# Sketched attention feeding a swish MoE on one core: query features spread over partitions through DRAM, a smaller first chunk, key sums on GpSimd, one fixed order

## The chip, the cores and the metric

The kernel runs on one core of one Trainium2 chip. The metric is device time in microseconds (us) of one execution; executions of one kernel mostly agree within a few per cent (130.0 to 135.0 us in all runs of the kernel before), and each comes with the mean clock that TensorE (PE) was granted, as a share of full speed. Lower is better. The engines are PE (matrix multiply), VectorE (DVE), ScalarE (ACT), GpSimd (POOL), and SyncE (SP), which issues most DMAs, the copies to and from DRAM. In these kernels data lies in SBUF, and PE's results in PSUM. A transfer lands when its last byte has arrived. A run is called slow when it is over 1.5% above the fastest run of its kernel; the others are fast.

## The reference

Four batches of four heads of 1088 tokens, head dimension 32. The attention is linear: each token's 32 values are projected by two 8 x 32 sketches, and phi is the outer product of the two results (64 features). Its output, 4352 tokens of 128 values, goes through a swish MoE layer with 2048 hidden units.

```python
def phi(x):
    a = np.einsum('rd,bhsd->bhsr', S1, x)
    b = np.einsum('rd,bhsd->bhsr', S2, x)
    return np.einsum('bhsi,bhsj->bhsij', a, b).reshape(*x.shape[:-1], 64)
q_p, k_p = phi(q), phi(k)
kv  = np.einsum('bhsf,bhsd->bhfd', k_p, v)
z   = np.sum(k_p, axis=2)
num = np.einsum('bhsf,bhfd->bhsd', q_p, kv)
den = np.einsum('bhsf,bhf->bhs', q_p, z)[..., None] + 1e-06
x   = (num / den)                       # then (tokens, 128)
h   = x @ w_in                          # 128 -> 2048
out = (h / (1 + np.exp(-beta * h))) @ w_out
```

## The kernel before

The MoE is cut into *waves*: PE multiplies two blocks of 128 hidden units with 512 tokens (tile `wave`, two buffers), ScalarE applies Silu to 128 x 1024 elements (tile `g`), and PE adds them into `moeout`. There are 68 of them. Attention work stands between the waves: phi(q) has 64 features on partitions, so PE *spreads* both sketch factors, each value repeated eight times, into PSUM (`aps`, `bps`). ScalarE copies one to SBUF (`asb`) and VectorE multiplies the two (`qp`). phi(k) has tokens on partitions: one burst `kps`, a transpose `kab`, and a product `kp` for each head; `kvz` holds kv and z, `dps` the denominator, `nps` the numerator. The divide writes `xT`, which the waves read.

```python
def ab(a_of=None, b_of=None, pool_b=None):      # spread for one pair of heads
    ...                                         # [cut: 8 or 16 matmuls into aps, bps]
    if a_of is not None:
        nc.scalar.copy(out=ASB[a_of][:, :, :w], in_=aps[:, :, :w])
    if b_of is not None:
        def mult():
            nc.vector.tensor_tensor(out=QP[bb][...], in0=bps[:, :, :w], in1=ASB[b_of][:, :, :w], op=MUL)

def sum_z(b):                                   # kp summed over its nine groups of tokens
    nc.vector.tensor_tensor(out=z4, in0=kp[:, :, 1:5], in1=kp[:, :, 5:9], op=ADD)
    ...                                         # [cut: three smaller adds]

for b in range(1, B):                           # later batches, each step between waves
    turn_q(b, 1)
    slot(lambda: r_group((b, 1, 0), (b, 0, 0)), 1)
    zs = sum_z(b)
    slot(lambda: kv(b, [1, 2, 3, 4], zs), 1 if few else 2)
    slot(lambda: r_group((b, 0, 1), (b, 1, 0)), 1)
    ...                                         # [cut: the same for the other parts, den, num, divide]
```

For each engine but SyncE the program fixes the order of its instructions: the one in which it names them. Beta is broadcast to 128 partitions by a DMA of 1 MB.

## Time and profile before

| | before |
|---|---|
| median of 3 runs, us | 131.4 (130.27 to 131.69) |
| first Silu, us from the span's start | 23.0 |
| second divide of batch 0 | 31.1 |
| first divide of batches 1, 2, 3 | 52.1, 77.2, 98.9 |
| end of the last Silu | 125.0 |
| DMA | 12.4 MB |

The first lines are from the page of the profile: the span of 130.2 us in 40 equal slices, each digit the busy share of a slice in tenths; PEclk is the granted clock, and DMA the mean share of 16 DMA engines.

```profile
PE   5787999887889999999997999999999989888830
...
ACT  1303010876358767477777866687776798888930
...
PEclk9999999999999999999999999999999999999998
DMA  3999999999992320031000400500032050031232
```

The next are from the table of stretches. For each stretch it has its length, then the busy us of PE, PE's weight loads, DVE, ACT and POOL (with the number of instructions), then granted clock, DMA share and GB/s.

```profile
core 0: us, PE busy (x) PEld busy (x) DVE busy (x) ACT busy (x) POOL busy (x), PEclk, DMA share, GB/s
0.00:23.00 23.00, 18.98 (x248) 8.77 (x248) 12.49 (x36) 3.55 (x8) 8.75 (x20) 1.00 0.96 270
23.00:57.00 34.00, 30.80 (x378) 11.05 (x382) 27.29 (x49) 22.84 (x27) 2.33 (x5) 1.00 0.58 122
57.00:102.00 45.00, 42.84 (x501) 16.65 (x501) 28.83 (x54) 32.97 (x38) 0.00 (x0) 1.00 0.17 25
102.00:125.00 23.00, 19.90 (x96) 9.11 (x95) 2.23 (x4) 20.41 (x21) 0.00 (x0) 1.00 0.23 35
```

PE is busy 31 of 34 us in the second stretch and 43 of 45 in the third, at full clock, and ScalarE 20.4 of 23 in the fourth. VectorE is busy 27 of 34 us in the second. The chain of work that ended last, followed backwards and given as shares by engine, says the same: PE and VectorE, hardly any DMA.

```profile
PE 49%; DVE 22%; ACT 15%; DMA 5%; issue 5%; SPq 1%; ACTq 0%; DVEq 0%
```

### The profile page before, as it was taken

What the parts mean: (1) busy time and instruction counts of PE and PEld (TensorE: products, weight loads), DVE (VectorE), ACT (ScalarE), POOL (GpSimd) and SP (SyncE); (2) the same over time, 40 slices, a digit from 0 to 9 for tenths busy, and PEclk for the clock granted to TensorE, in tenths of its full rate; (3) what the DMA queues carried; (4) which work ended last, traced back from release to release, by engine and by line L of the source; (5) the groups of instructions that cost most, each with busy time, mean ns of one, the idle gap of its engine ahead of it and who ended that gap; (6) DMA issues with size and microseconds to landing.
All of it is one profiled execution on the core that took longest, in us unless ns stands there. A gap on an engine that the chain in (4) does not pass through costs nothing.

```text
span 130.2 us, 2977 instructions
## 1 busy us (share of the span) xinstructions
PE 113.1 (87%) x1216; PEld 45.9 (35%) x1216; DVE 71.3 (55%) x142; ACT 79.8 (61%) x92; POOL 11.1 (9%) x24
## 2 busy tenths in 40 slices
PE   5787999887889999999997999999999989888830
PEld 2132933222334342342432332443432333334620
DVE  2579119249799988997367579940737400200210
ACT  1303010876358767477777866687776798888930
POOL 3000399700000000000000000000000000000000
PEclk9999999999999999999999999999999999999998
DMA  3999999999992320031000400500032050031232
GB/s 110 304 187 275 358 353 314 208 249 203 235 210 83 56 30 0 5 54 29 5 0 10 71 5 0 81 0 5 0 49 36 0 80 1 0 58 25 35 48 40
DMA packets 24909, 12.42 MB, mean 95 GB/s; under 512 B 18992, under 2 KB 23104, under 8 KB 24896
## 3 DMA queue, kind: packets, MB, share of 16 engines
q1 hardware_dynamic: 24576, 12.19, 42.1%
q8 instruction: 9, 0.15, 0.5%
q10 hardware_dynamic: 320, 0.04, 0.2%
q14 instruction: 4, 0.03, 0.1%
HBM read 10.00 MB, written 2.23 MB: 94 GB/s over the span
## 4 chain that ended last, share of the span: by engine, by line
PE 49%; DVE 22%; ACT 15%; DMA 5%; issue 5%; SPq 1%; ACTq 0%; DVEq 0%
PE moeout L223 15%; ACT g L267 15%; PE wave L259 13%; PE kvz L406 5%; DMA q<-in_q_dram 5%; PE aps L369 4%; DVE kp L346 4%; PE dps L471 3%; DVE qp L388 3%; PE bps L369 2%; DVE rb L489 2%; DVE xT L516 2%; PE nps L506 2%; PE kps L327 2%; DVE qT L315 2%
## 5 line engine op out<-in xcount | busy, mean ns | idle before, releaser
L267 ACT ACTIVATE g<-wave 128x1024 f16<-128x1024 f32 x68 | 67.8, 1023 | 30.1 <-PE wave L259 29.7
L223 PE MATMUL moeout<-g,woutp 128*128 128x512 f16 (+1 forms) x144 | 40.1, 369 | 3.3 <-ACT g L267 3.1
L259 PE MATMUL wave<-xT,winp 128*128 128x512 f16 (+1 forms) x144 | 40.0, 367 | 0.6 <-ACT g L267 0.4
L223 PEld LDWEIGHTS <-woutp 128*128 128x128 f16 x144 | 11.4, 97 | 24.8 <-issue 18.8
L259 PEld LDWEIGHTS <-winp 128*128 128x128 f16 x144 | 13.8, 97 | 17.3 <-issue 3.4
L388 DVE TENSOR_TENSOR qp<-bps,asb 128x576 f32<-128x576 f32 (+1 forms) x16 | 11.3, 713 | 14.5 <-ACT g L267 8.8
L233 DVE STREAM_TRANSPOSE o_sb<-moeout 128x512 f32<-128x512 f32 (+1 forms) x9 | 6.1, 676 | 21.5 <-PE moeout L223 21.5
L369 PE MATMUL aps<-qT,s_165 32*64 32x288 f32 (+1 forms) x128 | 13.6, 448 | 3.1 <-ACT g L267 2.0
L379 ACT COPY asb<-aps 128x576 f32<-128x576 f32 (+1 forms) x16 | 9.8, 610 | 5.7 <-PE aps L369 4.6
L369 PE MATMUL bps<-qT,s_170 32*64 32x288 f32 (+1 forms) x128 | 12.1, 446 | 0.1
L346 DVE TENSOR_TENSOR kp<-kab 128x576 f32<-128x576 f32 (+2 forms) x20 | 11.6, 620 | 0.0
L406 PE MATMUL kvz<-kp,v 128*32 128x64 f32 (+1 forms) x288 | 9.1, 246 | 1.2 <-DVE qp L388 0.8
L147 PE MATMUL warm<-idle 128*128 128x512 f16 x23 | 7.6, 479 | 1.5 <-DVE hm L159 1.5
L369 PEld LDWEIGHTS aps<-qT,s_165 32*64 32x64 f32 x128 | 4.6, 138 | 10.5 <-ACT g L267 5.3
L406 PEld LDWEIGHTS kvz<-kp,v 128*32 128x32 f32 (+1 forms) x288 | 6.5, 124 | 4.5 <-issue 2.3
L516 DVE TENSOR_TENSOR xT<-nps,rb 128x576 f16<-128x576 f32 (+1 forms) x8 | 5.8, 722 | 1.8 <-PE nps L506 1.4
L190 POOL TENSOR_TENSOR winp<-w_in_sb,beta_bc 128x256 f16<-128x256 f32 x8 | 5.5, 721 | 13.6 <-DMA beta_bc<-in_moe_beta_dram 13.6
L482 DVE STREAM_TRANSPOSE dT<-dps 128x288 f32<-128x288 f32 (+1 forms) x8 | 3.7, 463 | 5.1 <-PE dps L471 5.1
L315 DVE STREAM_TRANSPOSE qT<-q 128x576 f32<-128x576 f32 (+1 forms) x8 | 5.8, 726 | 0.8 <-DMA q<-in_q_dram 0.8
L489 DVE STREAM_TRANSPOSE rb<-rc 128x576 f32<-128x576 f32 (+1 forms) x8 | 6.0, 745 | 0.3
L327 PE MATMUL kps<-kT,sk 64*32 64x288 f32 x64 | 3.9, 482 | 2.3 <-DVE kT L303 2.3
L506 PE MATMUL nps<-qp,nd 64*32 64x288 f32 (+1 forms) x128 | 5.5, 401 | 0.0
(56 smaller groups left out, 60.9 us busy)
## 6 DMA issues: line engine op xcount, KB each, us to landing
v<-in_v_dram SPq DMA_DIRECT2D x16, 144.0 KB, 9.2
k<-in_k_dram SPq DMA_DIRECT2D x3, 544.0 KB, 11.8
q<-in_q_dram SPq DMA_DIRECT2D x3, 544.0 KB, 11.0
out_dram<-o_sb SPq DMA_DIRECT2D x20, 64.0 KB, 2.0
w_in_sb<-in_moe_w_in_dram SPq DMA_DIRECT2D x2, 512.0 KB, 8.7
beta_bc<-in_moe_beta_dram SPq DMA_DIRECT2D x2, 512.0 KB, 9.3
w_out_sb<-in_moe_w_out_dram SPq DMA_DIRECT2D x2, 512.0 KB, 9.8
k<-in_k_dram SPq DMA_DIRECT2D x1, 288.0 KB, 2.8
```

Of the source, the lines that this page charges most:

```text
L223: nc.tensor.matmul(out=moe["acc"][:, :tw], lhsT=woutp[:, j, :], rhs=g[:, jj, :tw], start=(j == 0), stop=(j == NJ - 1),)
L259: nc.tensor.matmul(out=wv[:, jj * tw : (jj + 1) * tw], lhsT=winp[:, (j0 + jj) * P : (j0 + jj + 1) * P], rhs=xT[:, t0 : t0 + tw], start=Tru ...
L267: nc.scalar.activation(out=g, in_=wv, func=ACTF.Silu)
L315: nc.vector.transpose(out=qT_of[b][:, t0 : t0 + tn].rearrange("p t c s -> p (t c s)"), in_=q_t[b][:, 2 * t0 : 2 * (t0 + tn)].rearrange("p ...
L346: nc.vector.tensor_tensor(out=KP[b][:, h, j0:j1].rearrange("p j (i l) -> p j i l", i=R), in0=bass.AP(tensor=a0.tensor, offset=a0.offset, a ...
L369: nc.tensor.matmul(out=dst[64 * c : 64 * c + 64, m, : 32 * tn], lhsT=sx[rows, :], rhs=qT_of[bb][rows, t0 : t0 + tn, c, :], start=True, sto ...
L379: nc.scalar.copy(out=ASB[a_of][:, :, :w], in_=aps[:, :, :w])
L388: nc.vector.tensor_tensor(out=QP[bb][:, 2 * pr : 2 * pr + 2, 32 * t0 : 32 * t0 + w], in0=bps[:, :, :w], in1=ASB[b_of][:, :, :w], op=MUL,)
L406: nc.tensor.matmul(out=kvz[32 * h : 32 * h + 32, F * which : F * which + F], lhsT=v_t[b][:kr, h, j, :] if which == 0 else ones[:kr, :], rh ...
L489: nc.vector.transpose(out=rb[:, :tn].rearrange("p t c s -> p (t c s)"), in_=bass.AP(tensor=r0.tensor, offset=r0.offset, ap=[list(r0.ap[0]) ...
L506: nc.tensor.matmul(out=nps[32 * h : 32 * h + 32, c, :w], lhsT=ND[b][rows, 32 * h : 32 * h + 32], rhs=QP[b][rows, h, 32 * t0 : 32 * t0 + w] ...
L516: nc.vector.tensor_tensor(out=xT[:, o : o + 2 * w].rearrange("p (t c s) -> p c t s", c=2, s=32), in0=nps[:, :, :w].rearrange("p c (t s) -> ...
```

## The change

The intent is to take work off PE and VectorE while the DMA queues stand mostly idle (DMA digits of 0 to 5 in the second half). For batches 1 to 3 the two small factors of phi(q) are computed unspread in one burst (`qps`), copied (`qsb`) and written to DRAM (`qd`). Reads with repeated addresses bring them back spread over 128 partitions (`qe`), and VectorE multiplies the two. Batch 0's first chunk has 256 tokens, its second 832, so there are 72 waves: 4 of 256 tokens, 16 of 416, the rest of 512 or less. The kp sums and nine of twelve kp products of later batches go to GpSimd. PE broadcasts beta. The order of all engines, SyncE included, is one string of tokens.

```diff
-    q_chk = [(0, 9), (9, TP - 9)]
+    q_chk = {b: [(0, 9), (18, 8)] for b in range(B)}
+    q_chk[0] = [(0, 4), (8, 13)]
+    tok_chk = [(0, 256), (256, 416), (672, 416)]        # then 512s
...
+    def qps(b):
+        t = two("qps")
+        ...                                             # 8 matmuls, unspread
+        nc.scalar.copy(out=s, in_=t[:, :, : NJK * 32])
+        nc.sync.dma_start(out=d, in_=s.rearrange("p a w -> p (a w)"))      # qd, in DRAM
+        for n in range(2):
+            nc.sync.dma_start(                          # first factor: one read, 128 partitions
+                out=e[0].rearrange("p m a w -> p (m a w)"),
+                in_=bass.AP(tensor=d.tensor, offset=d0 + 64 * n * W, ap=[[4 * W, 16], [0, R], [1, 2 * W]]))
+            for c in range(2):                          # second factor: two reads, 64 partitions
+                nc.sync.dma_start(
+                    out=e[1][64 * c : 64 * c + 64].rearrange("p m a w -> p (m a w)"),
+                    in_=bass.AP(tensor=d.tensor, offset=d0 + (64 * n + 32 * c + 2) * W,
+                                ap=[[0, R], [4 * W, R], [1, 2 * W]]))
+    def qmul(b, n, m=None):
+        nc.vector.tensor_tensor(out=QP[b, n][:, ms], in0=e[0][:, ms], in1=e[1][:, ms], op=MUL)
...
     def sum_z(b):
-        nc.vector.tensor_tensor(out=z4, in0=kp[:, :, 1:5], in1=kp[:, :, 5:9], op=ADD)
+        eng = nc.gpsimd
+        eng.tensor_tensor(out=z4, in0=kp[:, :, 0:4], in1=kp[:, :, 4:8], op=ADD)
...
+    SEQ = """
+        a0b1 lv2 tk1 c0 W a1 c1 mB1 b0 mB0 tq1 lk3 dB iB qp1 W W nB xB W W kp1 ka1 o12 o13 W W
+        W W tk2 tq2 W W O11 W W O10 kp2 va1 W m10 W tk3 z1 W vb1 ka2 np1 W lq3 nz1 m11 qp2 W d1
+        ...                                             # [cut: three more lines; W is one wave]
+    """
```

(Cut: the beta broadcast, other names, the order of the loads.)

The two reads of `qe` differ. The source pattern of the first factor has 16 rows as its outermost dimension, that of the second has a repeat of 8 with stride 0.

## The prediction

> **What bounds it now (131.4 us).** ScalarE's timeline splits the run by its 68 Silu waves of 1.02 us.
> - 0 to 23.0 us: prologue. The DMA row is full; the chain of waits runs q load, transpose, kab, kp, then kvz at 12.87 us. The page names a DVE multiply, but I read the v load there. kvz to 16.9, then kvd, nd, den, reciprocal, divide, wave.
> - 23 to 57 us: 18 waves, 1.9 us each. The table of stretches has DVE busy 8.9 to 9.4 of each 10 us from 30 to 60: DVE-bound.
> - 57 to 102 us: 29 waves, 1.55 us each, PE busy 8.8 to 9.9 of 10: PE-bound. PE needs 0.87 us for a wave's four 512-column matmuls, plus attention.
> - 102 to 125 us: 1.10 us a wave, ScalarE-bound. Tail 5.2 us.
>
> **Removed.**
> - Per later batch, four bursts of 16 spread matmuls (about 2.8 us) become one burst like kps (0.72): PE saves about 6 us in all. Four asb copies (2.4 us) become one of 0.64: ScalarE saves 5.3. The four PSUM products (2.85 us) become two of 1152 elements, estimate 1.35 us each from the 1024-element add of 1.21: nothing saved.
> - DVE loses the kp sums (2.75 us a batch) and 9 of 12 kp products (0.74 each): about 15 us.
> - The 1 MB broadcast of beta leaves the saturated prologue; PE and two ScalarE copies make it. Less q lies in front of v.
>
> **Added.** About 7.1 MB of DRAM reads and 0.9 MB of writes. From the 290 to 380 GB/s seen, about 7 us per batch plus two landings; small stores land in 2.0 us here[...]. GpSimd: at 721 ns per 256 elements, a kp product costs about 1.6 us and a batch's sums about 5.7 (estimates), 31 us in all, mostly off the chain.
>
> **Where it lies on the path (estimates).**
> 1. Prologue: v about 10.8, kv done about 13.4, 128-column chain, but the second chunk's spread stands before the first wave on PE: first Silu about 18.3 (before 23.0).
> 2. Waves 2 to 4 wait behind qps of batch 1 on PE, which waits for q's load (about 21.3). Second chunk divided about 27; batch 0 is then complete (before: 31.8).
> 3. Its 16 waves of 832 columns, about 1.0 us each, end about 43. Batch 1's second spread read, queued behind q, v, k loads, lands about 40, its divide about 45.5: a short gap.
> 4. 32 waves with batches 2 and 3: PE 0.87 x 32 + 5.6 x 2 = 39 us; with before's 10% slack about 43 us, to 89 us.
> 5. 20 waves ScalarE-bound, 21 us, then tail about 4.4 (last store on two queues).
> Sum: **114 us, range 107.5 to 121.** Faster by over 2%: 0.95; within 2%: 0.04; slower: 0.01.
>
> **What would show it.** First Silu at 17 to 19.5 us; no wave for some us before 24 and near 45; in the middle 1.3 to 1.4 us a wave; DVE under 65 us busy, GpSimd about 40; DMA about 19 MB.
>
> **What would make it wrong.** Spread reads landing late and blocking DVE and PE, which run in a fixed order. [...] If middle waves reach 1.15 us, 108.

(Two passages are cut from it: what it compared its 2.0 us of a small store with, and one way to be wrong that its trace did not show. No term of the sum is among them: 89 + 21 + 4.4 us is still about 114. Its 0.87 us for a wave's four matmuls is read from the trace of the kernel before, where matmuls of 512 columns in a row start at 88.48, 88.70, 88.92 and 89.13 us, 0.216 apart.)

## The result

| | before | after | predicted |
|---|---|---|---|
| median, us | 131.55 (130.27 to 133.44, 4 runs) | 141.43 (140.17 to 142.38, 4 runs) | 114 (107.5 to 121) |
| first Silu | 23.0 | 24.6 | 17 to 19.5 |
| second divide of batch 0 | 31.1 | 36.1 | about 27 |
| first divide of batch 1 | 52.1 | 62.2 | 45.5 |
| first divide of batches 2, 3 | 77.2, 98.9 | 84.8, 106.4 | none |
| end of the last Silu | 125.0 | 136.4 | none |
| DVE, GpSimd busy | 71.3, 11.1 | 56.7, 38.8 | under 65, about 40 |
| DMA, MB | 12.4 | 19.3 | about 19 |

The change is slower: the ratio is 1.074, with a 95% interval of 1.061 to 1.087. Ratios here and below are the mean time of one kernel's fast runs over that of the other's in the same rounds, so they are not quite the ratios of the medians. The profiled execution took 142.4 us, 1.6% over the fastest; where times inside it are compared with those of another kernel, the time of that kernel's profiled execution is taken.

The same lines of the page (span 140.6 us):

```profile
PE   5989299369998976869997399993399989889870
...
ACT  2261042504768566225889158884027798898860
...
PEclk9999956856999999779999999999559999999998
DMA  2999999501589564849857349956700404004042
```

PE has slices of 2 and 3 in the prologue and three of 3 in the middle, the DMA row is now busy to slice 29, and before the tail the clock has four stretches at half speed (17.0 to 23.8, 27.3 to 34.1, 58.0 to 61.4 and 98.9 to 105.8 us in the record of the clock). Just before three of these PE was busy 0.2 of 2.9 us, 0.9 of 2.7 and 1.1 of 3.5; but before the one at 58.0 us it was busy 1.1 of 1.8, and 1.2 of 3.6 us from 77.3 to 80.9 brought no half clock. The table of stretches, cut at the first Silu and at the divides that let waves begin:

```profile
0.00:24.60 24.60, 19.42 (x290) 8.54 (x290) 12.10 (x42) 7.18 (x17) 11.97 (x31) 0.86 0.89 291
24.60:36.10 11.50, 8.20 (x70) 2.62 (x71) 5.48 (x8) 4.34 (x6) 0.00 (x0) 0.70 0.25 88
36.10:62.20 26.10, 22.46 (x240) 9.67 (x238) 16.27 (x22) 14.92 (x20) 17.15 (x13) 0.93 0.64 141
62.20:106.40 44.20, 35.07 (x391) 13.95 (x391) 18.20 (x30) 25.95 (x29) 9.66 (x10) 0.92 0.63 143
106.40:136.40 30.00, 26.48 (x140) 11.63 (x139) 4.22 (x6) 25.64 (x28) 0.00 (x0) 1.00 0.20 32
```

In the stretch from 62.2 to 106.4 us PE is busy 35 of 44 us. The last long stretch, ScalarE busy 25.6 of 30, is as predicted. The chain that ended last, by engine and by line:

```profile
DMA 35%; PE 31%; ACT 10%; DVE 10%; issue 6%; SPq 5%; ACTq 1%; DVEq 0%
DMA qe<-qd 30%; ACT g L352 8%; PE moeout L318 8%; PE wave L343 6%; PE dps L596 4%; SPq L494 3%; PE kvz L528 3%; DMA beta<-in_moe_beta_dram 2%; DVE qp L509 2%; PE bps L442 2%; PE aps L442 2%; DVE rc L615 2%; ACT asb L453 1%; DMA qd<-qsb 1%; 
```

Nearly a third of the span now hangs on the reads `qe<-qd`. From the view of the waits (engine and line, what it waited for, us in total, times, longest):

```profile
DVE qp L509 <- DMA qe<-qd: 16.1, 4, 5.6
...
PE kvz L528 <- issue: 2.8, 1, 2.8
```

VectorE waited 16.1 us for these reads, four times. For each batch, from the issue of the first read to the start of the second product, the timeline shows 19, 17 and 17 us (36.12 to 55.25, 60.42 to 77.64, 82.58 to 99.44).

PE's timeline of the first 35 us (start, us busy, operation, and in brackets the idle time before and what ended it) shows two more losses. PE stands 2.8 us inside `kvz` where the profile finds nothing that it waits for ("issue"). Then the second chunk goes through one PSUM buffer, PE to ScalarE to VectorE to PE:

```profile
14.02 0.28 PE L528 MATMUL kvz<-kp,v 128*32 128x64 f32 x5
17.06 0.64 PE L528 MATMUL kvz<-kp,v 128*32 128x64 f32 x11 [2.77 <-issue]
...
24.72 0.93 PE L442 MATMUL aps<-qT,s 32*64 32x416 f32 x8 [0.38 <-ACT asb L453]
27.68 1.66 PE L442 MATMUL bps<-qT,s 32*64 32x416 f32 x8 [2.03 <-DVE qp L460]
30.49 1.61 PE L596 MATMUL dps<-qp,zb 128*32 128x416 f32 x8 [1.15 <-DVE qp L460]
32.03 1.21 PE L472 MATMUL qps<-qT,sq 64*32 64x288 f32 x16
```

`bps` takes 1.66 us here and `aps` 0.93, since the clock is at half from 27.3 to 34.1 us. SyncE's timeline shows that its queue is in order too (lines that start on SPq are issues; the time is from the first to the last of a group):

```profile
40.13 15.32 SPq L302 DMA_DIRECT2D out_dram<-o_sb  x8
55.50 0.47 SPq L117 DMA_DIRECT2D q<-in_q_dram  x1
56.07 0.38 SPq L483 DMA_DIRECT2D qd<-qsb  x1
...
79.40 0.59 SPq L147 DMA_DIRECT2D v<-in_v_dram  x1
80.09 0.54 SPq L483 DMA_DIRECT2D qd<-qsb  x1
```

The write `qd` of batch 2 stands behind the stores of an output chunk, that of batch 3 behind seven loads of v. Their data (`qsb`) was ready at 54.4 and 75.7 us.

### The profile page after: what moved, and what is told of

It is laid out like the page before. It is cut to its first block, busy times and chain, and to the rows that moved or that the text cites. A ratio compares the mean times of both kernels' runs of the same rounds, so it can differ in the third digit from the quotient of the medians.

```text
span 140.6 us, 2827 instructions
## 1 busy us (share of the span) xinstructions
PE 112.1 (80%) x1132; PEld 46.7 (33%) x1132; DVE 56.7 (40%) x106; ACT 78.1 (56%) x95; POOL 38.8 (28%) x53
## 3 DMA queue, kind: packets, MB, share of 16 engines
q1 hardware_dynamic: 26320, 19.07, 53.6%
## 4 chain that ended last, share of the span: by engine, by line
DMA 35%; PE 31%; ACT 10%; DVE 10%; issue 6%; SPq 5%; ACTq 1%; DVEq 0%
DMA qe<-qd 30%; ACT g L352 8%; PE moeout L318 8%; PE wave L343 6%; PE dps L596 4%; SPq L494 3%; PE kvz L528 3%; DMA beta<-in_moe_beta_dram 2%; DVE qp L509 2%; PE bps L442 2%; PE aps L442 2%; DVE rc L615 2%; ACT asb L453 1%; DMA qd<-qsb 1%; DVE qp L460 1%
## 5 line engine op out<-in xcount | busy, mean ns | idle before, releaser
L352 ACT ACTIVATE g<-wave 128x1024 f16<-128x1024 f32 (+2 forms) x72 | 67.4, 974 | 33.9 <-PE wave L343 33.5
L318 PE MATMUL moeout<-g,woutp 128*128 128x512 f16 (+3 forms) x160 | 41.9, 356 | 7.8 <-ACT g L352 4.2
L343 PE MATMUL wave<-xT,winp 128*128 128x512 f16 (+3 forms) x160 | 42.4, 362 | 1.2 <-DVE xT L643 1.2
L318 PEld LDWEIGHTS <-woutp 128*128 128x128 f16 x160 | 14.5, 99 | 31.6 <-issue 24.2
L328 DVE STREAM_TRANSPOSE o_sb<-moeout 128x512 f32<-128x512 f32 (+3 forms) x10 | 6.3, 630 | 33.3 <-PE moeout L318 30.4
L427 POOL TENSOR_TENSOR kp<-kab 128x576 f32<-128x576 f32 x9 | 11.5, 1301 | 24.8 <-DVE kab L419 21.8
L509 DVE TENSOR_TENSOR qp<-qe,qe 128x1152 f32<-128x1152 f32 x6 | 8.7, 1443 | 19.5 <-DMA qe<-qd 16.1
L596 PE MATMUL dps<-qp,zb 128*32 128x288 f32 (+2 forms) x64 | 6.7, 511 | 8.1 <-DVE qp L509 6.8
L550 POOL TENSOR_TENSOR z<-kp 128x1024 f32<-128x1024 f32 x3 | 7.0, 2350 | 11.9 <-DVE kp L427 11.8
L528 PE MATMUL kvz<-kp,v 128*32 128x64 f32 x288 | 6.7, 238 | 2.8 <-issue 2.8
L631 PE MATMUL nps<-qp,nd 64*32 64x288 f32 (+3 forms) x128 | 6.3, 458 | 0.0
```

The costliest lines, as they stand in the source:

```text
L318: nc.tensor.matmul(out=moe["acc"][:, :tw], lhsT=woutp[:, j, :], rhs=g[jj], start=(j == 0), stop=(j == NJ - 1),)
L328: nc.vector.transpose(out=o_sb[:, :nt, :].rearrange("p t d -> p (t d)"), in_=moe["acc"][:, :tw])
L343: nc.tensor.matmul(out=wv[:, jj // per, o : o + tw], lhsT=winp[:, (j0 + jj) * P : (j0 + jj + 1) * P], rhs=xT[:, t0 : t0 + tw], start=True, ...
L352: nc.scalar.activation(out=g[:, :, :gw], in_=wv[:, :, :gw], func=ACTF.Silu)
L427: (eng or nc.vector).tensor_tensor(out=KP[b][:, h, j0:j1].rearrange("p j (i l) -> p j i l", i=R), in0=cut(a0, [[32, jn], [1, R], [0, R]]), ...
L509: nc.vector.tensor_tensor(out=QP[b, n][:, ms], in0=e[0][:, ms], in1=e[1][:, ms], op=MUL)
```

## The experiments

All ran on the chip. Runs of one group shared a chip and the runs of the kernel before, whose fast runs had means of 130.9, 131.2, 131.6, 131.1 and 131.0 us in the five groups.

### Group 1: what the reads, GpSimd and the spread itself cost

**e1_wide**, wrong numbers: the second factor is read as one transfer with the first factor's pattern.

```diff
-            for c in range(2):
-                nc.sync.dma_start(out=e[1][64 * c : 64 * c + 64]..., ap=[[0, R], [4 * W, R], [1, 2 * W]])
+            nc.sync.dma_start(out=e[1]..., ap=[[4 * W, 16], [0, R], [1, 2 * W]])
```

> The second factor's two reads of 64 partitions become one read of 128 partitions with the address pattern of the first factor (the numbers are wrong on purpose; bytes unchanged). Theory A (narrow reads: these reads leave half of the DMA engines idle and run slowly on the rest, and their landing paces batches 1 to 3): the span from first read issue to the multiply of the second chunk falls from 19, 17 and 17 us to 8 to 10 us per batch, and the time falls to 118 to 127 us. Rival B (the TensorE clock that was granted at half speed after idle stretches sets the time) and rival C (GpSimd's sums and products hold VectorE and kvz up): no more than 3 us gained, 137 us or more.

Measured: 126.5 us (mean of the fast runs), ratio 0.967 (0.953 to 0.981). The same bytes come, in 11.0, 10.4 and 10.4 us a batch from the first packet to the end of the last, against 15.4, 14.7 and 14.7 in the changed kernel. That is 4.3 us a batch, three times. From the first issue to the second product it is now 16, 12 and 12 us, still not the 8 to 10 expected. The stretches of e1_wide between the same events (the columns as above):

```profile
34.20:56.80 22.60, 20.77 (x240) 9.57 (x239) 15.10 (x21) 15.04 (x20) 13.73 (x11) 1.00 0.71 166
56.80:90.70 33.90, 32.60 (x391) 13.61 (x391) 18.99 (x31) 25.71 (x29) 14.25 (x12) 1.00 0.82 185
90.70:120.70 30.00, 26.46 (x140) 11.65 (x139) 4.21 (x7) 25.77 (x28) 0.00 (x0) 1.00 0.20 32
```

The second row is the one to compare with 62.20:106.40 of the changed kernel. ScalarE runs the same 29 instructions in 33.9 us instead of 44.2, and PE is busy 32.6 of them. VectorE waits 5.1 us for the reads, not 16.1, and the chain hardly goes through DMA any more:

```profile
DVE qp L508 <- DMA qe<-qd: 5.1, 3, 3.2
...
PE 61%; ACT 17%; DVE 7%; issue 5%; DMA 4%; SPq 2%; ACTq 0%
```

So some 14 us of the miss lie in how the second factor is read, not in its bytes: 14.5 by the means of the fast runs, and 13.8 in the stages that hold reads. (The profiles differ by 1.8 us more before the first read at 36.1 us; runs with the same prologue have their first Silu between 22.9 and 24.6.)

**e1_k16**, wrong numbers: still two reads of 64 partitions each, but with 64 source rows outermost.

```diff
-    ap=[[0, R], [4 * W, R], [1, 2 * W]]
+    ap=[[W, 64], [1, 2 * W]]
```

> The second factor's two reads keep 64 partitions and the number of DMAs, but the source's outermost dimension is 64 rows instead of a repeat of 8 (wrong numbers on purpose). It parts two forms of theory A. If the count of DMA engines is the limit, the DMA row stays above 0.9 while reads run, a batch's reads take 11 to 13 us instead of 17 to 19, and the time is 126 to 134 us. If the 64 partitions alone are the limit, nothing changes: 138 us or more. Rivals B and C: no change.

Measured: one fast run of 126.35 us and three slow ones of 129.0 to 132.7; the packets of a batch took 10.3 to 11.0 us in the fast one. The two half-width destinations are therefore not what is slow; the outermost dimension of 8 is, in reads that SyncE issues (14.7 to 15.4 us a batch in the changed kernel). (This edit drops the repeat of addresses as well; e1_pool below keeps every address, and its packets are as fast, so the repeat alone is not the cause.) Below are 2 us near the end of a batch's reads in the changed kernel, where only narrow ones are left, and 2 us of e1_k16's reads (the columns as above): the DMA share is 0.54 against 1.04, and the rate 130 against 230 GB/s. A packet of 4.6 KB takes 0.32 us in the one and 0.34 in the other, so about half as many engines work at the same pace each (an estimate from the shares: 8.6 of 16, against all of them). Why these reads keep only half of them busy is not shown.

```profile
48.00:50.00 2.00, 1.85 (x10) 0.83 (x9) 1.67 (x2) 1.26 (x2) 1.18 (x2) 1.00 0.54 130
...
42.00:44.00 2.00, 1.88 (x16) 0.86 (x23) 0.00 (x0) 1.74 (x4) 1.99 (x1) 1.00 1.04 230
```

**kp_on_vector**: all kp products and sums of later batches back on VectorE, nothing else.

```diff
-            DO[f"o{b}{h}"] = lambda b=b, h=h: outers(b, [h], nc.gpsimd)
+            DO[f"o{b}{h}"] = lambda b=b, h=h: outers(b, [h], nc.vector)
...
-        eng = nc.gpsimd
+        eng = nc.vector
```

> The changed kernel with all kp products and sums back on VectorE. Rival C: faster by 5 us or more, since the 2 us stall of VectorE's add at 58 us and the wait for GpSimd's sums go. Theory A and rival B: within 2 per cent of the changed kernel (139 to 144 us), since VectorE is busy only 57 of 141 us and waits for the reads.

Measured: 141.0 us, ratio 1.078 (1.062 to 1.093), with VectorE busy 67.9 us and GpSimd 12.1. GpSimd's part is neither the cause nor a gain while the reads are slow.

**pe_spread**: later batches spread on PE as before, in the changed kernel's order.

```diff
-            DO[f"m{b}{n}"] = lambda b=b, n=n: qmul(b, n)
+            for pr in range(2):
+                DO[f"S{b}{n}{pr}"] = lambda b=b, n=n, pr=pr: spread_late(b, n, pr)   # ab, asb copy, product
```

(The string has S10, S11 and so on in place of m10, qp1 and so on.)

> phi(q) of batches 1 to 3 is spread on PE again, as in the kernel before, all else of the change kept (first chunk, GpSimd sums and products, beta by PE, fixed order). Theory A: no DRAM wait is left; 114 to 122 us, faster than the kernel before. Rival B: the prologue's half clock stays, so 133 us or more. Rival C: GpSimd's part stays, so slower than the kernel before (over 131 us).

Measured: 144.4 us, ratio 1.103 (1.087 to 1.120): a miss for theory A. The time lies in the ranges of rivals B and C, but neither is its cause by the other runs: e1_wide gained 14 us with GpSimd's part kept and most of the prologue's half clock too (17.1 us at half before 32 us), and kp_on_vector gained nothing. PE is busy 122.7 us and VectorE waits for the copy in 11 of the 12 spreads:

```profile
DVE qp L473 <- ACT asb L470: 23.2, 11, 3.1
```

The spread and the order can't be taken apart so simply. An order made for one big product a half batch is a bad one for four small chains. This run says nothing of what DRAM costs.

### Group 2: mending the reads, the clock, half of the spread, and sums alone

**e1_pool**: one word changed. GpSimd issues the second factor's reads.

```diff
             for c in range(2):
-                nc.sync.dma_start(
+                nc.gpsimd.dma_start(
                     out=e[1][64 * c : 64 * c + 64].rearrange("p m a w -> p (m a w)"),
```

> The changed kernel, correct, with the second factor's reads issued by GpSimd instead of SyncE; same addresses and sizes. If a read issued there is dealt to all 16 DMA engines whatever its outermost dimension (theory A then predicts the wide time): DMA row full while reads run, 127 to 134 us. If it is dealt to 8 as well: 139 to 145 us, no better than the change.

Measured: correct, 130.9 us, ratio 0.9975 (0.987 to 1.008). The packets of a batch took 10.1 to 11.1 us, as in e1_wide, with the outermost dimension still 8. The trace has a DMA share of 1.03 from 42 to 44 us. Why the issuing engine makes this difference is not shown. Issuing a batch's four reads held GpSimd for 2.25 us, about 0.56 each. This is the useful form of the same test, as its numbers are right, and it gains about 10 us on the changed kernel. It is 4 us short of e1_wide. In the profiles 1.5 us of that lie before the first Silu, where there are no reads, and 2.7 between the first divides of batches 2 and 3 (16.1 us against 13.4). Why is open. GpSimd's waits do not show that its products and sums hold the reads up:

```profile
POOL qe L494 <- DMA qd<-qsb: 16.9, 2, 13.6
...
POOL qe L494 <- DVE rc L617: 7.8, 1, 7.8
```

GpSimd's queue is in order (a kp product of batch 3, whose `kab` was written by 62.3 us, ran at 78.42, behind the reads issued from 76.19, though GpSimd had been idle for 3.3 us), but it sat idle before each batch's reads until the write had landed. The wait put down to `rc` is such a one too: SyncE's first read of that batch was issued at 55.8 us and GpSimd's at 56.3.

**wide_warm**: e1_wide with six dummy matmuls in the second chunk's chain.

```diff
-        a0b1 lv2 tk1 c0 W a1 c1 mB1 b0 mB0 tq1 lk3 dB iB ...
+        a0b1 lv2 tk1 c0 W a1 w3 c1 mB1 b0 w3 mB0 tq1 lk3 dB iB ...
```

> The wide-read kernel (wrong numbers, as e1_wide) plus six 512-column dummy matmuls on PE: three behind the spread of the second chunk's first factor and three behind that of its second, where PE was idle for 2.0 and 1.1 us and the clock was then at half for 6.8 us. If the half clock is a term of the loss (rival B as a second cause): the window of half clock from 25 to 32 us goes, the second chunk's divide comes 2 to 3 us earlier than at 34.2 us, and the time falls by 1.5 to 3 us against e1_wide (124 to 126). If only the chain's length counts: within 1 us of e1_wide.

Measured: 126.1 us, ratio 0.961 (0.949 to 0.973), so 0.4 us from e1_wide by these means, in other rounds; clock 0.986 instead of 0.929. The second chunk's chain is some 1.7 us earlier, and in the two profiled executions (125.0 and 126.8 us) that lead lasts to the end. The intervals overlap, so the half clock in that chain is worth at most about 2 us, and perhaps nothing.

**half_dram**: only the first factor goes through DRAM (with four buffers), the second is spread on PE.

```diff
-            for c in range(2): ...                      # the narrow reads
+    def bmul(b, n, pr):
+        bps = two("bps")
+        ab([("b", (n, pr), bps)], b)
+        nc.vector.tensor_tensor(out=QP[b, n][:, :, pr, :w], in0=bps[:, :, :w], in1=QE[b, n][0][:, :, pr, :w], op=MUL)
```

> A correct kernel without the narrow reads: the first factor comes through DRAM (rows as the outermost dimension, 128 partitions), the second is spread by PE into PSUM as in the kernel before and multiplied there; four buffers for the reads. Theory A: two reads a batch of 590 KB land within 5 to 7 us of the first issue; PE gets about 1.4 us a batch more than in e1_wide; 124 to 131 us, so equal to or up to 5 per cent faster than before. If any DRAM round trip is too slow in this order: over 135 us.

Measured: 137.8 us, ratio 1.050 (1.036 to 1.063), a miss. The wait for reads has become a wait for PE's bursts, which stand behind waves:

```profile
DVE qp L501 <- PE bps L442: 18.2, 12, 5.3
```

**before_zpool**: the kernel before with its kp sums on GpSimd, nothing else.

```diff
-        nc.vector.tensor_tensor(out=z4, in0=kp[:, :, 1:5], in1=kp[:, :, 5:9], op=ADD)
+        nc.gpsimd.tensor_tensor(out=z4, in0=kp[:, :, 1:5], in1=kp[:, :, 5:9], op=ADD)
```

> The kernel before with one part of the change alone: the kp sums on GpSimd. If VectorE bounds the stretch from 23 to 57 us as I read it, taking 2.75 us a batch off it saves 1.5 to 4 us (127 to 130). If the sums' longer latency on GpSimd (about 5.2 us, feeding the kvz products) costs as much, it is within 1 per cent.

Measured: 132.7 us, ratio 1.011 (0.996 to 1.027). VectorE was busy 63.7 us instead of 71.3, and nothing came of it. So the reading of the stage from 23 to 57 us as VectorE-bound is not confirmed: VectorE is busy there, but taking sums from it gained nothing. Whether VectorE was not the limit, or the sums' longer time on GpSimd took the gain back, this run does not part.

### Group 3: the prologue and the first chunk, on top of e1_pool

**late_loads**: seven loads, which nothing needs before about 22 us, wait until batch 0's last kp product (about 13 us), in a slightly changed order.

```diff
-    load_win(DFF // 2, DFF)
-    load_rows(k, k_t, 1, "k")
-    ...                                                 # and five more
     nc.gpsimd.tensor_copy(out=gate, in_=KP[0][:, H - 1, NJK - 1, :1])
+    nc.gpsimd.memset(w_in_sb[:, DFF // 2 : DFF // 2 + 1], 0.0)   # the load that follows must wait for this
+    load_win(DFF // 2, DFF)
+    load_rows(k, k_t, 1, "k")
+    ...
```

> The version with the second factor's reads issued by GpSimd (130.8 us), with seven loads that nothing needs before about 22 us (second half of w_in and w_out, k and q of batches 1 and 2, v of batch 1) held back until the last kp product of batch 0, about 13 us. Open: PE stops inside kvz of batch 0 for 2.4 to 3.8 us in every run and the trace shows nothing that it waits for; a 16 KB packet of an instruction fetch ends about 1.3 us before it goes on. Theory A, the fetch stands behind the queued loads: PE's gap falls below 1.5 us, the first Silu comes at 21.5 to 22.5 us instead of 24.6, time 128 to 129.5. Theory B, the gap has nothing to do with the loads: gap still 2.4 to 3.8 us, first Silu at 24 to 25, time 130 to 132.

Measured: 127.9 us, ratio 0.972 (0.966 to 0.978). PE's gap in `kvz` fell from 3.8 us (e1_pool) to 1.5, the first Silu came at 22.1 us instead of 24.6, and all that follows kept its pace and came 2.5 us earlier. PE's timeline of late_loads around the gap:

```profile
14.04 0.28 PE L521 MATMUL kvz<-kp,v 128*32 128x64 f32 x5
15.81 0.41 PE L521 MATMUL kvz<-kp,v 128*32 128x64 f32 x11 [1.49 <-issue]
```

In the packet records, a 16 KB packet of an instruction queue ends at 15.8 us in the changed kernel, 16.3 in e1_pool and 14.4 here, and PE goes on at 17.1, 17.7 and 15.8, each time 1.2 to 1.5 us later; so it is in all 15 profiles that have the gap. The moment at which PE goes on says more than the gap's length: in chunk512 below, with all loads queued, the gap is 1.3 us, but PE goes on at 17.1, as in the changed kernel. That the queued loads delay PE there is shown by this run. That PE waits there for instructions is a reading: it fits these and the later runs, but no run varied the fetch alone.

**early_waves**: the three waves left of the first chunk and batch 1's qps burst (in a buffer of the waves) stand in the idle time of the second chunk's chain.

```diff
-        a0b1 lv2 tk1 c0 W a1 c1 mB1 b0 mB0 tq1 lk3 dB iB qp1 W W nB xB W W kp1 ...
+        a0b1 lv2 tk1 c0 W a1 W c1 tq1 qp1 mB1 b0 W mB0 lk3 W dB iB nB xB W W kp1 ...
```

> The same version (130.8 us) with its loads as they were, but the order in the second chunk's chain changed: the three waves left of the first chunk and the qps burst of batch 1 stand between the spread bursts, where PE and ScalarE wait for each other (about 6 us of idle PE between 24 and 30 us). Theory A, this idle time is part of what the prediction missed: four Silu before 30 us instead of one before 33, batch 1's write to DRAM lands about 31 instead of 35.8, time 127.5 to 129. Theory B, the second chunk's chain alone sets what follows, or the middle stage is bound by PE's fixed order: time 130 to 132.

Measured: 135.7 us, ratio 1.031 (1.020 to 1.042): 5 us worse than e1_pool, where theory A expected 2 to 3 better and theory B no change. The divide came at 37.1 instead of 35.2 us, because the waves stood before the chain on PE. Then one kp product of batch 1 (the second `kp` line; its `kab` was written by 41.6 us) stood behind the output transpose of a wave chunk on VectorE's timeline, and GpSimd's sum behind it:

```profile
43.89 0.71 DVE L427 TENSOR_TENSOR kp<-kab 128x576 f32<-128x576 f32 x1
47.45 0.62 DVE L328 STREAM_TRANSPOSE o_sb<-moeout 128x416 f32<-128x416 f32 x1 [2.84 <-PE moeout L318]
47.99 0.72 DVE L427 TENSOR_TENSOR kp<-kab 128x576 f32<-128x576 f32 x1
```

With one fixed order, a wave that is moved forward moves every later chunk's end against the attention steps.

**chunk512**: batch 0's chunks and the waves as before (576 tokens first, 68 waves).

```diff
-    q_chk[0] = [(0, 4), (8, 13)]
-    tok_chk = [(0, 256), (256, 416), (672, 416)]
+    tok_chk = [(0, 512)]                                # and three W moved into the chain
```

> The same version (130.8 us) with one part of the change undone: the first query chunk is 576 tokens and the waves are cut in 512s as before, so 68 waves and no waves of 832 columns. Theory A, the small first chunk starts the waves earlier and pays as predicted: undoing it costs 2 to 4 us, 132.5 to 135, with the first Silu about 26. Theory B, its gain is lost since only one of its four waves runs before 33 us: first Silu about 26 but three Silu before 32, no waves of 832 columns, time 128 to 131.

Measured: 133.0 us, ratio 1.011 (1.001 to 1.020), 2 us worse than e1_pool. The first Silu came at 24.1 us, though, not later. So undoing the small first chunk cost about 2 us, and not by a later start; since three waves were moved with it, how much of the 2 us is the chunk's own is open.

**all_three**: late_loads, early_waves' order, and the kp sums on VectorE.

```diff
+    # the edits of late_loads and early_waves
-        eng = nc.gpsimd
+        eng = nc.vector
```

> Held-back loads and the new order of the second chunk together, and the kp sums back on VectorE so that GpSimd's queue is free to issue the reads. Candidate for a version that beats both kernels. If both gaps of the prologue are real and their gains add: 123.5 to 127. If the middle is bound by PE's order: 128 to 131. VectorE busy about 63 us, first Silu about 22.

Measured: 133.7 us, ratio 1.022 (1.012 to 1.032), a miss. The order of early_waves (5 us lost) and the sums on VectorE (see early_z) both stand against the held-back loads; this run does not part them.

### Groups 4 and 5: the second chunk's chain, and whether the causes add

(early_spread_again, narrow_early and early_z are group 5.)

**early_spread**: on top of late_loads, the first two spread bursts of the second chunk run ahead of the first chunk's divide, in place of four warm-up matmuls. No wave is moved.

```diff
+    turn_q(0, QA0, 24)                                  # both while VectorE waits for kvz
+    turn_q(0, 24, T)
...
-    keep_warm(4)
+    spread(B0, B1)
     divide(0, 0, nps)
-    turn_q(0, 24, T)
```

> The version with held-back loads (127.9 us) with the first two spread bursts of batch 0's second chunk ahead of the first chunk's divide, where four warm-up matmuls stood, and the q transposes for them in VectorE's wait for kvz; no wave is moved against the rest. Theory A, the serial chain of batch 0 (first chunk, then second chunk through one PSUM buffer) is what the prediction missed besides the reads, and every us of it shifts all that follows: second chunk's divide about 2.4 us earlier (30.4 instead of 32.8), time 125 to 126. Theory B, the order further on or PE sets the pace: divide earlier, time within 0.7 us of 127.9.

Measured: one fast run of 124.7 us, slow ones of 127.5 and 129.4, and one of 239.3 us at full clock, which nothing explains. It was run again:

> The same kernel as early_spread, whose fast state had one run only (124.7 us; another took 239 us at full clock, which nothing explains). If the earlier spread is worth its 2.4 us: fast runs at 124.5 to 126, against 127.9 with the held-back loads alone. If the one fast run was chance: 127 to 128.5.

Measured, on another chip: fast runs of 126.2 and 127.8 us, four slow ones of 128.3 to 131.4, ratio 0.971 (0.959 to 0.984). Against the kernel before this is the ratio of late_loads (0.972), so of the 2.4 us expected the fast runs do not show a sure gain. Whether the earlier spread by itself gains is left open.

**early_k**: as early_spread, and batch 1's kps burst (in a buffer of the waves), its transposes and GpSimd's products stand in the second chunk's chain.

```diff
-        ... W a1 c1 mB1 b0 mB0 tq1 lk3 dB iB qp1 W W nB xB W W kp1 ka1 o12 o13 W W
+        ... W a1 c1 kp1 mB1 b0 ka1 o12 o13 mB0 tq1 lk3 dB iB qp1 W W nB xB W W W W
```

> As early_spread, and batch 1's kps burst, its transposes and GpSimd's two products stand in the second chunk's chain, where PE and VectorE wait. If holes in that chain are worth what fits in them: kps leaves the busy stretch, 0.5 to 1.5 us better than early_spread, 124 to 125.5. If the delayed chain costs more than that: the second chunk's divide about 1 us later than in early_spread, time 126 to 127.5.

Measured: correct, 125.0 us (median 125.3 of 4 runs), ratio 0.953 (0.941 to 0.965). This is the fastest correct version: 4.7% faster than the kernel before. Its first Silu is at 18.6 us, the second divide of batch 0 at 29.5, batch 1's first at 50.8.

**wide_early**, wrong numbers: e1_wide, late_loads and early_spread together.

```diff
+    # the edits of e1_wide, late_loads and early_spread
```

> Wrong numbers on purpose: the changed kernel with wide reads of the second factor (127.0 us), held-back loads and the earlier spread together. If the causes named so far add (reads 14, held-back loads 2.9, earlier spread 2.4): 121 to 122.5, so about 7.5 us of the prediction's miss are left to the middle's pace. If the two prologue gains are lost behind the reads: 123.5 to 126.5.

Measured: two fast runs of 123.4 and 123.5 us, two slow ones of 125.5 and 126.3. That is 3.0 us below e1_wide. 5.3 had been expected, but 2.4 of these were the earlier spread's, which early_spread_again did not show; late_loads alone had gained 3.0 on e1_pool. So the held-back loads' gain adds in full, and no gain of the earlier spread is seen in the total.

**narrow_early**: the changed kernel with its narrow reads, late_loads and early_spread.

```diff
+    # the edits of late_loads and early_spread; the reads stay on SyncE, two of 64 partitions with 8 outermost
```

> The changed kernel with its narrow reads issued by SyncE as they were, and held-back loads and the earlier spread alone. If the causes are independent and add: about 5.3 us better than the changed kernel, 135 to 137 against 141.4. If the narrow reads take the prologue's gain back: 138.5 to 141.5. If the held-back loads also bring batch 1's reads into full queues: over 141.

Measured: 133.5 to 140.9 us, median 137.5 of 6 runs, one of them fast. The median is 4 us below the changed kernel's, but it is one of slow runs, and with one fast run and such a spread it decides nothing. Its time goes with the granted clock: 0.920 in the run of 133.5 us, 0.886 in that of 140.9.

**early_z**: early_k with the kp sums on VectorE.

```diff
-        eng = nc.gpsimd
+        eng = nc.vector
```

> As early_k, with the kp sums on VectorE, so that GpSimd's in-order queue, which also issues the reads, is free sooner. If that queue still holds batches 2 and 3 back: 0.5 to 2 us better than early_k, 123 to 124.5. If VectorE's order takes it back, as with all_three: 125 to 127.

Measured: 129.8 us, ratio 0.994 (0.982 to 1.005), against early_k's 0.953 (0.941 to 0.965) on another chip, so the sums' place on GpSimd is right in this order. The waits have PE standing 5.7 us for VectorE's sum: VectorE's order takes it back.

## Why the prediction was wrong

The times of the events, in the profiled executions (us from the start of the span; the last row is the whole time):

| | predicted | changed | e1_wide | wide_early |
|---|---|---|---|---|
| first Silu | 18.3 | 24.6 | 23.1 | 19.4 |
| second divide of batch 0 | 27 | 36.1 | 34.2 | 31.0 |
| first divide of batch 1 | 45.5 | 62.2 | 56.8 | 53.6 |
| from there to the end | 68.5 | 80.2 | 70.0 | 69.8 |
| time | 114 | 142.4 | 126.8 | 123.4 |

The difference of each pair of columns, row by row, is how far a stage is off. From the prediction to e1_wide the miss is 12.8 us: 4.8 to the first Silu, 2.4 more to batch 0's second divide, 4.1 more to batch 1's first, and 1.5 after it. From e1_wide to the changed kernel it is 15.6: 1.5, 0.3, 3.6 and 10.2.

- **The reads: the step that failed.** The prediction put "about 7 us per batch plus two landings" for 2.4 MB a batch, at the 290 to 380 GB/s of the plain loads. It was 17 to 19 us from the first issue to the second product (12.4 with wide reads, in batches 2 and 3). Two things were mis-sized. The second factor's reads have 8 as their outermost dimension and, issued by SyncE, ran at a DMA share of 0.54: 14.7 to 15.4 us of packets, against 10.3 to 11.0 with 16 or 64 outermost (e1_wide, e1_k16) and 10.1 to 11.1 with 8 issued by GpSimd (e1_pool). And even those 10.4 us are over 7: 2.4 MB in 10.4 us is some 230 GB/s. The diff showed the 8; the prediction took the rate of the prologue's loads for these reads too, and no run had been made to check it. The narrow reads are worth about 14 us of 27.
- **"Spread reads landing late and blocking DVE and PE, which run in a fixed order"** was named as what would make the prediction wrong. That is what happened: VectorE waited 16.1 us for `qe`. The chance given to it, 0.01 for slower, was far too small.
- **The prologue (first Silu 18.3).** Wrong by 4.8 to 6.3 us. The 1 MB of beta left the queues, and PE still stood in `kvz` for 2.8 us with nothing visible to wait for; holding loads back cut the same gap from 3.8 to 1.5 us in late_loads. The other terms were small: PE's beta broadcast took 2.0 us and kps 1.25. kv was done at 17.7 us and not at 13.4; the other 2 us or so lie behind it. With these loads held back and the spread moved, wide_early came within about 1 us of the predicted first Silu.
- **The second chunk "about 27".** The prediction had waves 2 to 4 wait for a load of q. In the trace no transpose of q waited for its load there. The chunk goes through one PSUM buffer, each step waiting for another engine's (`bps` stood 2.0 us for VectorE's product, `dps` 1.2), with the clock at half from 27.3 us. From the first Silu to the divide it took 11.5 us (24.6 to 36.1) and not 8.7.
- **"Its 16 waves of 832 columns, about 1.0 us each", with batch 1 in 18.5 us.** Even with wide reads it was 22.6 us (34.2 to 56.8), with PE busy 20.8 of them: batch 1's attention work (`kps` 2.4, a burst taking 1.18 with its new pattern and 0.72 in the kernel before; `kvz` 1.5, `dps` 1.2, `qps` and `nps` 0.7 each) had been left out of PE's time. This term was 4 us short.
- **The middle at 1.3 to 1.4 us a wave, the ScalarE-bound end and the tail** were right once the reads were wide: 26 waves took the 33.9 us from 56.8 to 90.7, 1.30 each, and from batch 1's first divide to the end e1_wide took 70.0 us where the prediction's terms give 68.5.
- **VectorE relieved of 15 us.** It was relieved (56.7 us busy, 71.3 before), but no gain of that is shown: before_zpool and kp_on_vector moved 8 to 11 us of its work and changed nothing. Once the reads are mended it can matter: early_z put the sums back on VectorE and lost about 5 us. The product of 1152 elements took 1.36 us, as estimated (1.35); the two of the changed kernel that overlapped GpSimd's work took 1.60 and 1.62.
- **VectorE beside GpSimd.** One VectorE operation of 36 elements took 2.17 us at 58.2 us, beside 0.20 elsewhere, while GpSimd's sum ran from 57.98 to 60.33. What held it up is not shown. It is rare here: taking GpSimd's work away gained nothing (kp_on_vector, 141.0 us).
- **The half clock.** Not in the prediction. The changed kernel has 23.9 us of half clock before its tail where the kernel before has none. Filling one stretch (wide_warm) was worth at most about 2 us. Where the half clock follows a wait for reads, its share of the 14 us was not separated, but it can be bounded: from 36.1 to 106.4 us the changed kernel's PE is busy 57.5 us, and in the same two stages of e1_wide, with as many instructions and the clock at full, 53.4. So about 4 of the 14 us are the most that the slower clock can have added there (an estimate from the two tables of stretches).

What stays open: what the earlier spread is worth, why e1_pool is slower than e1_wide between batches 2 and 3, and, of the 9.4 us between wide_early and the prediction, the parts outside batch 1's stage (1.1 to the first Silu, 2.9 in the second chunk, 1.3 at the end).

## What to carry to other kernels

DRAM reads of the same bytes can differ by their outermost dimension: issued by SyncE, a batch's packets took 14.7 to 15.4 us here with 8 outermost in the second factor's source, and 10.3 to 11.0 with 16 or 64. Before a change rests on such reads, time them in a run of their own, and take the one-word test of another issuing engine (10.1 to 11.1 us from GpSimd, with the 8 kept). When all engines have one fixed order, an experiment that moves work must not move what stands in front of what elsewhere: the same idea lost 5 us as early_waves, which moved waves, and is part of the fastest version as early_k, which moved none ahead. And a wait that the profile ascribes to nothing can still be bought back, as from 3.8 us to 1.5 in late_loads: look at what the DMA queues hold at that moment.
